# Retention attention ahead of two dense layers: quarter-array attention blocks and a finer share of dense work

## The chip, the cores and the metric

One Trainium2 chip, one core. The metric is device time in microseconds (us) for one execution of the whole program. TensorE (PE) multiplies, VectorE (DVE), ScalarE (ACT) and GpSimd (POOL) work on elements, SyncE (SP) issues most of the transfers.

## The reference

Three layers follow each other. The first is attention with a state that decays per head (batch 2, 8 heads, 768 tokens, 64 values per head); its output, 1536 tokens of 512 values, passes through two dense layers.

```python
state = gamma * state + k_t (outer) v_t          # per head, gamma = 1 - 2**(-5 - h)
y_t = (1 / sqrt(64)) * q_t @ state
...
h = x @ w_in;  x = (h * tanh(softplus(h))) @ w_out              # 512 -> 2048 -> 512
x = (sigmoid(x @ w_gate) * (x @ w_val)) @ w_out                 # 512 -> 1536 -> 512
```

All inputs and the output are float32.

## The kernel before

**Attention by blocks.** The 1536 tokens are 12 blocks of 128 (six for each batch). `load` brings `qk` and `nv` of a block (512 KB each), four blocks ahead. `at_prep` lets GpSimd scale the values (`vp`) and, except for the first block of a batch, the table of output scales (`og`). `at_scores` multiplies keys with queries, 64 rows of the array for each of the two heads of a pair and 128 outputs (`sc`), and VectorE masks the result (`a`). `at_state` adds keys times values into a state bank (`st`, K = 128 rows, 64 outputs), which ScalarE copies to `s` for the next block. `at_out` adds masked scores times values (`ao<-a,vp`, "inside") and queries times state (`ao<-qk_t,s`, "across", head 0 on rows and outputs 0 to 63, head 1 on 64 to 127) in one bank, and VectorE scales it into the layer's input `acc`. Each attention product is f32 and stands in the trace as two matmul instructions.

**Dense work.** A dense product of f32 accuracy is three matmuls with operands that are split in a rounded part and a remainder (`mm3`): ScalarE writes the rounded part, VectorE or GpSimd the remainder (`split`, `put`). Weights arrive packed (`raw`, 512 KB a piece) and are decoded by two ScalarE and two VectorE operations (`decode`). `plain1(i, c)` computes two tiles of the first layer for a chunk of 512 tokens; each tile is twelve matmuls of 512 columns. `mish` is ScalarE's activation, `put_g` splits its result.

**Order.** While `early` holds, every engine's queue follows the order of the Python calls. `blocks` goes through four attention blocks: scores of block j + 1, one step of weight preparation (`pump`), state and output of block j, the next loads, and then one dense tile. Chunk 0 is complete after block 3 (`put_plain` makes its split copies `xc`), chunk 1 after block 7 (`put_block`, `B11` and `B21`). So no dense work runs beside blocks 0 to 3, and one tile of twelve matmuls follows each of the eight later blocks. `flush` emits the rounded parts and remainders of weights that are due. After block 11 `early` is cleared: the rest of the program is recorded as a graph and `replay` issues it in an order found by list scheduling. Its first work is `out1(0, 0, G0)`, 48 matmuls with the weights `wo`; beside it GpSimd and ScalarE form the sums and differences of blocks (`T`, `B`, `YT`) which the later products need.

Of the kernel before, what the change touches and what calls it, by code (L numbers as in the profile page):

```python
# [23 lines left out]
def kernel(ctx, tc, qk, nv, w1i, w1o, w2g, w2v, w2o, ma_in, og_in, sg_in, ck_in, out):  # L24
# [26 lines left out]
    AHEAD = 4  # L51

# [213 lines left out]
    y_t = {n: big.tile([P, 2, 2, H], F32R, name="Y" + n) for n in ("T1", "T2", "T3")}  # L266
    y_t |= {"B11": xc_t[:, :2, :, :H], "B21": xc_t[:, 2:, :, :H], "T4": xc_t[:, :2, :, H:], "B22": xc_t[:, 2:, :, H:]}
# [47 lines left out]
    steps, late_hi, late_lo, sums_t, vs = [], [], [], {}, {}  # L315
# [51 lines left out]
    def put(key, v):  # L367
        t = slot(key)
        if home(key) == "q":
            v = v[:, H:]  # L370
        hi, lo = t[:, 0], t[:, 1]
        late_hi.append(lambda: act.activation(out=hi, in_=v, func=AF.Copy))
# [43 lines left out]
    def flush():  # L416
        flush_hi()
        while late_lo:
            late_lo.pop(0)()

    def pump(n=1):
        flush()
        for _ in range(n):
            if not steps and not plan():
                return
            ring = steps[0][0]
            if not room(ring) if ring else "dcs" not in lo_eng:
                return
            steps.pop(0)[1]()

    def weight(key):
        while key not in w_t:
            if not steps:
                assert plan(), key
            steps.pop(0)[1]()
        flush()
        return w_t[key]
# [45 lines left out]
    g_t = {}  # L483
# [94 lines left out]
    def plain_steps(key, done, halves=None, own=False):  # L578

        def one(i):  # L580
            o = hx["pool"].tile([P, N], F32, tag=f"x{i}", name="hx") if own and i in hx["own"] else hbank()
            w = weight(("a", *key, i))
            for kk in range(KK):
                xs, k = (xc_t, kk) if not halves else (b_t[halves[kk // 2]], kk % 2)
                mm3(o, lambda a: w[:, a, kk * P:kk * P + P], lambda b: xs[:, k, b, :], kk == 0, kk == KK - 1)
            spend(("a", *key, i))
            r[i] = o
            done(i, r)

        r = {}  # L590
        return [lambda: one(0), lambda: one(1)]

    def put_g(e, key):
        g = gp.tile([P, 2, N], F32R, tag="g", name="g")
        split(e, g[:, 0], g[:, 1], lo_eng["g"])
        g_t[key] = g

# [14 lines left out]
    def o1(i, c, d, k=2):  # L612
        o = hbank() if i == c == 0 else ps_o.tile([P, N], F32, tag="o", name="o")
# [63 lines left out]

    def out2(j, c):
        return seq([lambda s=s: o2(j, c, s) for s in range(SPC)])
# [27 lines left out]
    with ExitStack() as actx:  # L707
        ac = actx.enter_context(tc.tile_pool(name="ac", bufs=1))
        ld = actx.enter_context(tc.tile_pool(name="ld", bufs=AHEAD))
        at = actx.enter_context(tc.tile_pool(name="at", bufs=2))  # L710
        ps_s = actx.enter_context(tc.tile_pool(name="ps_s", bufs=1, space=PSUM))
        hx["pool"], hx["own"] = actx.enter_context(tc.tile_pool(name="ps_e", bufs=1, space=PSUM)), (0,)
        ma = ac.tile([P, 1, P], F32, name="ma")
        ck = ac.tile([P, SPB, 2 * NP, 1], F32, name="ck")
        sg = ac.tile([P, SPB, NP, 1], F32, name="sg")
        og0 = ac.tile([P, NP, P], F32, name="og0")
        qk_t, nv_t, a_t, vp_t, og_t, st_t, s_t = {}, {}, {}, {}, {}, {}, {}
# [8 lines left out]
        def at_prep(j):  # L726
            if j >= NSUB:
                return
            vp_t[j] = at.tile([P, 2 * NP, D], F32, tag="vp", name="vp")
# [3 lines left out]
            og_t[j] = og0  # L733
            if j % SPB:
                og_t[j] = at.tile([P, NP, P], F32, tag="og", name="og")
                pool.tensor_tensor(out=og_t[j], in0=og0, in1=sg[:, j % SPB].to_broadcast([P, NP, P]), op=ALU.mult)

        def at_scores(j):
            t = qk_t[j]
            sc = [ps_h.tile([P, NP, P], F32, tag="h", name="sc") for _ in range(2)]  # L740
            for p in range(NP):
                for e in range(2):
                    r = slice(D * e, D * e + D)
                    pe.matmul(out=sc[e][:, p, :], lhsT=t[r, 1, p, :], rhs=t[r, 0, p, :])
            a = at.tile([P, 2, NP, P], F32, tag="a", name="a")
            for e in range(2):
                dve.tensor_tensor(out=a[:, e], in0=sc[e], in1=ma.to_broadcast([P, NP, P]), op=ALU.mult)
            a_t[j] = a

        def at_out(j):  # L750
            a, v, t, s = a_t.pop(j), vp_t[j], qk_t[j], s_t.get(j)
            o = ps_o.tile([P, NP, P], F32, tag="o", name="ao")
            inter = j % SPB > 0

            for p in range(NP):
                for e in range(2):
                    pe.matmul(
                        out=o[D * e:D * e + D, p, :], lhsT=v[:, 2 * p + e, :], rhs=a[:, e, p, :],
                        start=p == 0, stop=p == NP - 1 and not inter, skip_group_check=True,
                    )  # L760
            if inter:
                for p in range(NP):
                    for e in range(2):
                        r = slice(D * e, D * e + D)
                        pe.matmul(
                            out=o[r, p, :], lhsT=s[r, p, :], rhs=t[r, 0, p, :], start=False, stop=p == NP - 1,
                            skip_group_check=True,
                        )
            dve.tensor_tensor(
                out=acc_t[j // SPC][:, :, j % SPC * P:j % SPC * P + P], in0=o, in1=og_t[j], op=ALU.mult  # L770
            )

        def at_state(j):
            if j % SPB == SPB - 1:
                return
            v, k = vp_t[j], nv_t[j]
            if j % SPB == 0:
                st_t[0] = ps_s.tile([P, NP, D], F32, tag="s", name="st")
            st = st_t[0]
            for p in range(NP):  # L780
                for e in range(2):
                    pe.matmul(
                        out=st[D * e:D * e + D, p, :], lhsT=k[:, 0, 2 * p + e, :], rhs=v[:, 2 * p + e, :],
                        start=j % SPB == 0 and p == 0, stop=p == NP - 1, skip_group_check=True,
                    )
            s_t[j + 1] = at.tile([P, NP, D], F32, tag="s", name="s")
            act.activation(out=s_t[j + 1], in_=st, func=AF.Copy)

        def fin(j):
            at_state(j)  # L790
            at_out(j)

        def blocks(j0, dense, made):

            for j in range(j0, j0 + SPC):
                if j + 1 < NSUB:
                    at_scores(j + 1)
                if j >= SPC - 1:
                    pump()
                fin(j)  # L800
                flush_hi()
                at_prep(j + 2)
                load(j + AHEAD)
                load_piece()
                if j == j0 + SPC - 1:
                    flush()
                    made()
                if dense:
                    dense.pop(0)()
            run(dense)  # L810

        for t, table in ((ck, ck_in), (ma, ma_in), (og0, og_in), (sg, sg_in)):
# [3 lines left out]
        z = at.tile([P, NP * D], F32, tag="s", name="z")  # L816
        dve.memset(ap=z, constant=0.0)
        for n in range(WARM):
            o = ps_o.tile([P, NP * D], F32, tag="o", name="warm")
            pe.matmul(out=o, lhsT=z[:, 0:P], rhs=z)  # L820
        for j in range(AHEAD):
# [4 lines left out]
        blocks(0, [], put_plain)  # L826
        blocks(SPC, plain1(0) + plain1(1), lambda: (put_block("B11", 1, 0), put_block("B21", 1, 2)))
        blocks(2 * SPC, plain1(0, 1) + plain1(1, 1), lambda: None)
# [8 lines left out]
    for n in ("T4", "B22", "T1", "T2", "T3"):  # L837
        b_t[n] = big2.tile([P, 2, 2, N], F32R, tag=n, name=n)

    put_block("T4", 2, 0)  # L840
    put_block("B22", 2, 2)
    run(side_sums(), out1(0, 0, G0))
# [38 lines left out]
def _tables(H, D, S, C):  # L881
# [3 lines left out]
    ma = np.arange(C)[None, None, :] >= np.arange(C)[:, None, None]  # L885
    pos = np.arange(S).reshape(S // C, C) - S // 2
# [4 lines left out]
    tables = (("ma", ma), ("og", og), ("sg", sg), ("ck", ck[..., None]))  # L891
# [42 lines left out]
```

## Time and profile before

| | |
|---|---|
| median of 3 timed runs | 591.86 us (591.84 to 592.0) |
| the profiled execution | 592.67 us, span 590.5 us |
| PE busy | 578.4 us (98%), 3342 matmul instructions |
| PE weight loads | 483.4 us (82%), beside the matmuls |
| DVE, ACT, POOL busy | 387.0 (66%), 294.9 (50%), 401.2 us (68%) |
| moved by DMA | 52.30 MB |
| granted TensorE clock, mean | 0.999 |

The page's first part gives the busy time of each engine; a busy PE is one with a matmul in flight, which does not mean that the array is full. The page cuts the span into 40 slices of 14.76 us: DMA is at 9, 9 and 7 tenths in the first three and at 4 tenths or less afterwards. Views used below: tables of busy time by stretch (with the count of instructions in brackets), instructions in order of time (runs of equal ones merged, with the idle time before them and what ended it), and groups of instructions with their mean duration.

### The profile page before, as it was taken

The numbers are of one execution on the slowest core, as the hardware profiler recorded it, in microseconds if no ns is written. First come the engines' busy times: TensorE is split into PE (matmuls) and PEld (weight loads), VectorE is DVE, ScalarE is ACT, GpSimd is POOL, SyncE is SP. The second block draws the span as 40 slices with busy tenths as digits, with TensorE's granted clock in tenths as the row PEclk, the third lists the DMA queues.
The fourth block names the chain that finished last, engine by engine and source line by source line (L and its number), as shares of the span: only waits on it lengthen the run. The fifth ranks groups of instructions, "written<-read, shape, count | busy, mean of one in ns | idle before, by whom it ended". The sixth has DMA issues, their size and how long they took to land.

```text
span 590.5 us, 8781 instructions
## 1 busy us (share of the span) xinstructions
PE 578.4 (98%) x3342; PEld 483.4 (82%) x3342; DVE 387.0 (66%) x540; ACT 294.9 (50%) x533; POOL 401.2 (68%) x344
## 2 busy tenths in 40 slices
PE   8999999999999999999999999999999999999997
PEld 6788878778888888888778778788888888888885
DVE  3899730167878775748883657887677677654564
ACT  1455556466666655346655556575254354340220
POOL 3566299999995846258999998997484484560120
PEclk9999999999999999999999999999999999999999
DMA  9974320023323231203220022333222222000004
GB/s 344 404 273 147 108 73 0 1 71 103 108 94 127 71 108 40 68 2 117 91 78 1 0 72 72 108 108 107 72 72 72 72 71 72 0 2 1 0 37 178
DMA packets 15593, 52.30 MB, mean 89 GB/s; under 512 B 1984, under 2 KB 2112, under 8 KB 15552
## 3 DMA queue, kind: packets, MB, share of 16 engines
q1 hardware_dynamic: 14976, 51.39, 25.2%
q8 instruction: 26, 0.43, 0.3%
q10 hardware_dynamic: 576, 0.36, 0.2%
q14 instruction: 15, 0.12, 0.1%
HBM read 48.60 MB, written 3.15 MB: 88 GB/s over the span
## 4 chain that ended last, share of the span: by engine, by line
PE 79%; POOL 10%; DMA 3%; DVE 3%; issue 2%; ACT 1%; SPq 0%; DVEq 0%; POOLq 0%; ACTq 0%
PE o L143 33%; PE h L143 27%; PE hx L143 16%; POOL t L143 3%; PE ao L143 2%; POOL g L143 2%; DMA raw<-w1i 2%; POOL T L143 2%; PE sc L143 1%; DMA qk_t<-qk 1%; POOL s L143 1%; POOL YT L143 1%; POOL B L143 1%; POOL ww L143 1%; PE st L143 1%
## 5 line engine op out<-in xcount | busy, mean ns | idle before, releaser
L143 POOL TENSOR_TENSOR g<-e,g 128x512 fp32r<-128x512 f32 x81 | 112.5, 1400 | 79.2 <-ACT g L143 74.6
L143 DVE TENSOR_TENSOR acc<-o,acc 128x512 f32<-128x512 f32 x132 | 90.8, 688 | 65.5 <-PE o L143 64.6
L143 PE MATMUL o<-g,wo 128*128 128x512 f32 x528 | 129.0, 393 | 0.2
L143 PEld LDWEIGHTS o<-g,wo 128*128 128x128 f32 x528 | 96.4, 188 | 21.8 <-DVE acc L143 2.6
L143 PE MATMUL o<-wo,g 128*128 128x512 f32 x432 | 108.8, 392 | 0.5 <-ACT acc L143 0.5
L143 PE MATMUL h<-B,ww 128*128 128x512 f32 x372 | 94.7, 391 | 0.1
L143 PE MATMUL h<-T,ww 128*128 128x512 f32 x360 | 91.9, 391 | 1.2 <-ACT acc L143 1.0
L143 PEld LDWEIGHTS o<-wo,g 128*128 128x128 f32 x432 | 78.1, 189 | 15.2 <-ACT acc L143 1.1
L143 POOL TENSOR_TENSOR ww<-s,ww 128x512 fp32r<-128x512 f32 x35 | 51.3, 1468 | 53.2 <-ACT ww L143 53.2
L143 DVE SCALAR_TENSOR_TENSOR raw<-raw 128x512 int32<-128x512 int32 x68 | 70.5, 1037 | 22.7 <-ACT raw L143 22.3
L143 PEld LDWEIGHTS h<-B,ww 128*128 128x128 f32 x372 | 68.7, 188 | 14.6 <-POOL B L143 0.5
L143 PEld LDWEIGHTS h<-T,ww 128*128 128x128 f32 x360 | 66.9, 188 | 16.6 <-ACT acc L143 1.5
L143 DVE SCALAR_TENSOR_TENSOR v<-v,raw 128x512 int32<-128x512 int32 x68 | 70.5, 1038 | 6.4 <-ACT v L143 3.9
L143 ACT ACTIVATE raw<-raw 128x512 int32<-128x512 uint8 x68 | 45.6, 673 | 42.8 <-DMA raw<-w2g 10.0
L143 ACT ACTIVATE e<-h 128x512 f32<-128x512 f32 x57 | 33.8, 593 | 58.0 <-PE h L143 35.7
L143 ACT ACTIVATE g<-e 128x512 fp32r<-128x512 f32 x84 | 51.7, 630 | 16.0 <-DVE e L143 14.8
L143 PE MATMUL hx<-xc,ww 128*128 128x256 f32 (+1 forms) x336 | 54.4, 299 | 1.1 <-DVE hx L143 0.8
L143 PEld LDWEIGHTS hx<-xc,ww 128*128 128x128 f32 x336 | 48.6, 190 | 6.7 <-DVE hx L143 1.2
L143 DVE TENSOR_TENSOR h<-h,u 128x512 f32<-128x512 f32 x54 | 37.6, 696 | 24.5 <-PE h L143 24.2
L143 ACT ACTIVATE v<-raw 128x512 f32<-128x512 f32 x68 | 44.9, 665 | 15.5 <-POOL s L143 11.3
L143 PEld LDWEIGHTS hx<-YT,ww 128*128 128x128 f32 x288 | 40.6, 190 | 7.5 <-DVE u L143 2.6
L143 PE MATMUL hx<-YT,ww 128*128 128x256 f32 x288 | 42.3, 283 | 2.7 <-DVE u L143 1.8
(80 smaller groups left out, 735.6 us busy)
## 6 DMA issues: line engine op xcount, KB each, us to landing
raw<-w1i SPq DMA_DIRECT2D x16, 512.0 KB, 3.3
raw<-w1o SPq DMA_DIRECT2D x16, 512.0 KB, 3.4
qk_t<-qk SPq DMA_DIRECT2D x12, 512.0 KB, 6.2
nv_t<-nv SPq DMA_DIRECT2D x12, 512.0 KB, 7.1
raw<-w2g SPq DMA_DIRECT2D x12, 512.0 KB, 3.3
raw<-w2v SPq DMA_DIRECT2D x12, 512.0 KB, 3.4
raw<-w2o SPq DMA_DIRECT2D x12, 512.0 KB, 3.4
out<-acc SPq DMA_DIRECT2D x12, 256.0 KB, 2.0
```

The costliest lines, as they stand in the source:

```text
L143: i = call(**kw)
```

## The change

A block from the fifth on is treated as two halves of 64 tokens: scores only inside a half, the state copied after every half, and "across" products with the state of the start of the batch to the half. Every product is then 64 rows, 64 outputs and 64 columns, a quarter of the array; the state and the scores of one half use the rows of that half, and the two heads of a pair the two halves of the outputs. In the host's layout and in the state the two heads of pairs 1 and 3 change places. `lanes` alternates products of two lists that lie on different row halves. The first four blocks keep whole blocks, but their "across" products use all four quarters in turn, on two banks.

The 32 quarter-tiles of dense work (three matmuls each) are shared out over nine rounds by `SHARE`. `load_piece` comes before the load of block 4, weight remainders go to GpSimd after block 4, the split of `g` is put off to the next round, the scale tables are made once for both batches, the split of chunk 0 is shared between VectorE and GpSimd, and the first 48 output products fill four banks in another order (`first1`).

```diff
+    SHARE = (4, 4, 3, 3, 2, 2, 4, 5, 5)
+    T = 4
...
-    y_t = {n: big.tile([P, 2, 2, H], F32R, name="Y" + n) for n in ("T1", "T2", "T3")}
...
-            split(acc_t[c][:, k0 + k], b_t[n][:, k, 0], b_t[n][:, k, 1], lo_eng["x"])
+            split(acc_t[c][:, k0 + k], b_t[n][:, k, 0], b_t[n][:, k, 1], pool if early and k0 else lo_eng["x"])
...
+        parts = [[lambda i=i, kk=kk: part(i, kk) for kk in range(KK)] for i in range(2)]
+        return parts[0] + parts[1] if early else [lambda s=s: run(s) for s in parts]
...
+        late_g.append(lambda: split(e, g[:, 0], g[:, 1], lo_eng["g"]))
+        if not early:
+            late_g.pop(0)()
...
+    def first1(c):
+        o = [hbank() for _ in range(KK)]
+        def part(m, d):
+            w, g = weight(("o", 1, m)), g_t[1, m, c]
+            mm3(o[d], lambda a: w[:, a, d * P:d * P + P], lambda b: g[:, b, :], m == 0, m == G0 - 1)
...
+        return seq([lambda m=m, d=d: part(m, d) for n in (0, 2) for d in range(KK) for m in (n, n + 1)])
...
+        def quarter(o, w, x, start=True, stop=True):
+            pe.matmul(out=o, lhsT=w, rhs=x, start=start, stop=stop, skip_group_check=True)
+        def scores(j, r):
...
+            def pair(p):
+                for s in range(2):
+                    quarter(sc[rows(s), p // 2, 2 * (p % 2) + (r + p) % 2, :], t[rows(r), 1, p, rows(s)],
+                            t[rows(r), 0, p, rows(s)])
+        def mask(j):
...
+            for r in range(2):
+                h = slice(r, NP - r, 3 - 2 * r)
+                dve.tensor_tensor(out=a[:, :, h], in0=sc_t.pop((j, r))[:, :, h, :],
+                                  in1=mh.to_broadcast([P, 2, NP // 2, Q]), op=ALU.mult)
+        def state(j, s):
...
+                for e in range(2):
+                    quarter(st[rows((e + p) % 2), p, :], k[rows(s), 0, 2 * p + e, :], v[rows(s), 2 * p + e, :],
+                            new and p == 0, p == NP - 1)
+        def keep(j, s):
+            s_t[2 * j + s + 1] = at6.tile([P, NP, D], F32, tag="s", name="s")
+            act.activation(out=s_t[2 * j + s + 1], in_=st_t[0], func=AF.Copy)
+        def outs(j, row):
...
+            def inside(p):
+                for e in range(2):
+                    quarter(o[rows(e), p, rows(row)], v[rows(row), 2 * p + e, :], a[rows(row), p // 2, 2 * (p % 2) + e, :],
+                            row == 0 and p == 0, False)
+            def across(p, s):
+                for m in range(2):
+                    quarter(o[rows((row + m) % 2), p + m, rows(s)], s_t[2 * j + s][rows(row), p + m, :],
+                            t[rows(row), 0, p + m, rows(s)], False, True)
...
+        def block(j, middle=lambda: None):
+            lanes(state(j + 1, 0) + scores(j + 1, 0), outs(j - 1, 1))
...
+            keep(j + 1, 0)
+            at_prep(j + 2)
+            middle()
+            while late_g:
+                late_g.pop(0)()
+            if j < NSUB - 1:
+                lanes(outs(j, 0), scores(j + 1, 1) + state(j + 1, 1))
+                mask(j + 1)
...
+            keep(j + 1, 1)
...
+        run(state(T, 0))
+        keep(T, 0)
+        lanes(scores(T + 1, 0), scores(T + 1, 1))
+        mask(T + 1)
+        run(state(T, 1))
+        keep(T, 1)
+        flush()
+        for k in range(KK):
+            split(acc_t[0][:, k], xc_t[:, k, 0], xc_t[:, k, 1], (dve, pool)[k % 2])
+        run(outs(T, 0), state(T + 1, 0))
+        keep(T + 1, 0)
+        at_prep(T + 2)
+        pump()
+        work(SHARE[0])
+        run(state(T + 1, 1))
+        keep(T + 1, 1)
+        load_piece()
+        lo_eng["w"] = pool
...
+        for j in range(T + 1, NSUB + 1):
+            block(j, lambda: (flush(), middles.get(j, lambda: None)()))
+            load(j + AHEAD - 1)
+            if j < NSUB and j != 2 * SPC:
+                feed()
+            work(SHARE[j - T])
...
-    run(side_sums(), out1(0, 0, G0))
+    run(side_sums(), first1(0))
```

## Rows read from the trace of the kernel before

**Rows 1.** The page's first part: engine, busy us, share of the span, instructions

```profile
PE 578.4 (98%) x3342; PEld 483.4 (82%) x3342; DVE 387.0 (66%) x540; ACT 294.9 (50%) x533; POOL 401.2 (68%) x344
```

**Rows 2.** Busy time by stretch: stretch, length, engines (count), clock, DMA share, GB/s

```profile
25.33:72.00 46.67, 46.35 (x483) 36.88 (x482) 42.61 (x54) 25.65 (x48) 24.19 (x18) 1.00 0.53 192
72.00:131.00 59.00, 56.51 (x257) 45.41 (x256) 17.43 (x19) 34.83 (x67) 56.85 (x53) 1.00 0.14 45
```

**Rows 3.** PE in order of time, one round: start us, us, operation, out<-in, shapes, count

```profile
47.31 1.16 PE L143 MATMUL sc<-qk_t 64*128 64x128 f32 x16
48.40 0.69 PE L143 MATMUL st<-vp,nv_t 128*64 128x64 f32 x16
48.91 1.05 PE L143 MATMUL ao<-a,vp 128*64 128x128 f32 x16
49.89 1.09 PE L143 MATMUL ao<-qk_t,s 64*64 64x128 f32 x16
50.91 3.01 PE L143 MATMUL hx<-B,ww 128*128 128x512 f32 x12
53.85 0.38 PE L143 MATMUL sc<-qk_t 64*128 64x128 f32 x2
```

**Rows 4.** Busy time by stretch, state group alone: first bracket counts matmuls in flight

```profile
41.94:41.95 0.01, 0.01 (x2) 0.01 (x4) 0.00 (x0) 1.00 1.99 819
41.96:41.96 0.00, 0.00 (x3) 0.00 (x5) 0.00 (x0) 1.00 0.00 0
41.97:41.98 0.01, 0.01 (x4) 0.01 (x6) 0.00 (x0) 1.00 0.00 0
42.02:42.03 0.01, 0.01 (x6) 0.01 (x6) 0.00 (x0) 1.00 0.00 0
```

**Rows 5.** The same for a scores group, with 128 columns

```profile
47.53:47.62 0.09, 0.09 (x4) 0.09 (x4) 0.00 (x0) 1.00 1.32 546
47.64:47.67 0.03, 0.03 (x6) 0.03 (x4) 0.00 (x0) 1.00 0.33 137
```

**Rows 6.** POOL in order of time, values of blocks 4 and 5 [idle before <-releaser]

```profile
18.89 1.04 POOL L143 TENSOR_TENSOR vp<-nv_t,ck 128x512 f32<-128x512 f32 x1 [2.07 <-DMA nv_t<-nv]
...
22.72 1.04 POOL L143 TENSOR_TENSOR vp<-nv_t,ck 128x512 f32<-128x512 f32 x1 [1.78 <-DMA nv_t<-nv]
```

**Rows 7.** PE in order of time, first dense product and the scores behind it

```profile
25.33 2.81 PE L143 MATMUL hx<-xc,ww 128*128 128x512 f32 x10
...
29.12 1.16 PE L143 MATMUL sc<-qk_t 64*128 64x128 f32 x16
```

**Rows 8.** PE in order of time, output products and the wait behind them

```profile
71.85 11.04 PE L143 MATMUL h<-g,wo 128*128 128x512 f32 x48
...
86.98 1.65 PE L143 MATMUL h<-T,ww 128*128 128x512 f32 x6 [1.03 <-ACT acc L143]
```

**Rows 9.** Groups of instructions, 25.3 to 72 us: busy us, mean ns | idle, releaser

```profile
L143 POOL TENSOR_TENSOR g<-e,g 128x512 fp32r<-128x512 f32 x7 | 10.0, 1424 | 14.5 <-ACT g L143 14.5
L143 DVE TENSOR_TENSOR a<-sc,ma 128x512 f32<-128x512 f32 x14 | 8.9, 677 | 0.0
...
L143 POOL TENSOR_TENSOR vp<-nv_t,ck 128x512 f32<-128x512 f32 x6 | 8.4, 1403 | 1.3 <-DMA nv_t<-nv 1.3
...
L143 ACT ACTIVATE g<-e 128x512 fp32r<-128x512 f32 x7 | 4.4, 631 | 0.2
...
L143 ACT ACTIVATE s<-st 128x256 f32<-128x256 f32 x6 | 2.2, 365 | 0.0
```

**Rows 10.** The tile nv_t from 30 us on: time from issue to landing

```profile
DMA to landing us min/median/max: 4.4/5.0/5.6
```

**Rows 11.** DVE and POOL in order of time, around the last block's end

```profile
71.00 0.68 DVE L143 TENSOR_TENSOR acc<-ao,og 128x512 f32<-128x512 f32 x1
...
73.45 1.29 POOL L143 TENSOR_TENSOR g<-e,g 128x512 fp32r<-128x512 f32 x1 [3.71 <-ACT g L143]
```

More of the change, by code (lines that the diff above doesn't have):

```diff
@@ new lines, in state, with pair @@
+        def state(j, s):
+            if j >= NSUB:
+                return [lambda: [quarter(st_t[0][rows(c), 0, :], z[rows(0), rows(0)], z[rows(0), rows(0)]) for c in range(2)]]
+            v, k = vp_t[j], nv_t[j]
+            new = j % SPB == 0 and s == 0
+            if new:
+                st_t[0] = ps_s.tile([P, NP, D], F32, tag="s", name="st")
+            st = st_t[0]
+            def pair(p):
+                for e in range(2):
+                    quarter(st[rows((e + p) % 2), p, :], k[rows(s), 0, 2 * p + e, :], v[rows(s), 2 * p + e, :],
+                            new and p == 0, p == NP - 1)
+            return [lambda p=p: pair(p) for p in range(NP)]
@@ new lines, in keep @@
+        def keep(j, s):
+            s_t[2 * j + s + 1] = at6.tile([P, NP, D], F32, tag="s", name="s")
+            act.activation(out=s_t[2 * j + s + 1], in_=st_t[0], func=AF.Copy)
+        def outs(j, row):
+            if not T <= j < NSUB:
+                return []
+            if row == 0:
+                o_t[j] = ps_o.tile([P, NP, P], F32, tag="o", name="ao")
+            a, v, t, o = a_t[j], vp_t[j], qk_t[j], o_t[j]
+            def inside(p):
[6 more added lines that the diff above has]
+                            t[rows(row), 0, p + m, rows(s)], False, True)
+            return [lambda p=p: inside(p) for p in range(NP)] + [
+                lambda p=p, s=s: across(p, s) for s in range(2) if (2 * j + s) % (2 * SPB) for p in (0, 2)]
@@ L750, in at_out @@
         def at_out(j):
-            a, v, t, s = a_t.pop(j), vp_t[j], qk_t[j], s_t.get(j)
-            o = ps_o.tile([P, NP, P], F32, tag="o", name="ao")
-            inter = j % SPB > 0
+            a, v, t, s = a_t.pop(j), vp_t[j], qk_t[j], s_t.get(2 * j)
+            o = [ps_o.tile([P, NP // 2, P], F32, tag="o", name="ao") for _ in range(2)]
             for p in range(NP):
@@ L782, in at_state @@
                     pe.matmul(
-                        out=st[D * e:D * e + D, p, :], lhsT=k[:, 0, 2 * p + e, :], rhs=v[:, 2 * p + e, :],
-                        start=j % SPB == 0 and p == 0, stop=p == NP - 1, skip_group_check=True,
-                    )
[L786 to L810, printed above, removed]
@@ L812, with lanes @@
-        for t, table in ((ck, ck_in), (ma, ma_in), (og0, og_in), (sg, sg_in)):
+                        out=st[rows((e + p) % 2), p, :], lhsT=k[:, 0, 2 * p + e, :], rhs=v[:, 2 * p + e, :],
+                        start=j == 0 and p == 0, stop=p == NP - 1, skip_group_check=True,
+                    )
+            s_t[2 * j + 2] = at6.tile([P, NP, D], F32, tag="s", name="s")
+            act.activation(out=s_t[2 * j + 2], in_=st, func=AF.Copy)
+        def lanes(*sides):
+            for n in range(max(map(len, sides))):
+                for side in sides:
+                    if n < len(side):
+                        side[n]()
@@ L813 @@
+        for t, table in ((ck, ck_in), (ma, ma_in), (og_t[0], og_in), (sg, sg_in), (mh, mh_in)):
             act.dma_start(out=t, in_=table)
@@ L820, with work, feed @@
             pe.matmul(out=o, lhsT=z[:, 0:P], rhs=z)
+        def work(n):
+            for _ in range(n):
+                dense.pop(0)()
+        def feed():
+            pump()
+            load_piece()
         for j in range(AHEAD):
@@ L825 @@
         at_scores(0)
-        blocks(0, [], put_plain)
-        blocks(SPC, plain1(0) + plain1(1), lambda: (put_block("B11", 1, 0), put_block("B21", 1, 2)))
-        blocks(2 * SPC, plain1(0, 1) + plain1(1, 1), lambda: None)
+        dense = plain1(0) + plain1(1) + plain1(0, 1) + plain1(1, 1)
+        for j in range(T):
+            at_state(j)
+            if j < T - 1:
+                at_scores(j + 1)
+            else:
+                lanes(scores(T, 0), scores(T, 1))
+                mask(T)
+            at_out(j)
+            if j == 0:
+                load_piece()
+            load(j + AHEAD)
+            if j:
+                load_piece()
+            at_prep(j + 2)
+            if j == T - 2:
+                pump()
+        flush_hi()
+        run(state(T, 0))
[4 more added lines that the diff above has]
+        keep(T, 1)
+        flush()
+        for k in range(KK):
[3 more added lines that the diff above has]
+        at_prep(T + 2)
+        pump()
+        work(SHARE[0])
+        run(state(T + 1, 1))
+        keep(T + 1, 1)
+        load_piece()
+        lo_eng["w"] = pool
+        middles = {2 * SPC: lambda: put_block("B11", 1, 0), 2 * SPC + 1: lambda: put_block("B21", 1, 2)}
+        for j in range(T + 1, NSUB + 1):
[4 more added lines that the diff above has]
+            work(SHARE[j - T])
+        flush()
+        lo_eng["g"] = dve
+        while late_g:
+            late_g.pop(0)()
+        assert not dense
         flush()
```

109 lines of the change are left out of this document (66 added, 43 removed).

## The prediction

> **What bounds the kernel now.** I read the engine table of the page first, then a table of engine time by stretch, then TensorE's instructions in order of time, then what VectorE, ScalarE and GpSimd wait for. The table says PE (TensorE) is busy 98% of the span [rows 1], and by stretch it is busy 46.35 of the 46.67 us from the first dense product to 72 us; in the next 59 us it lacks only 2.5 us [rows 2]. So the end is set by how much PE work there is; the other engines matter where they are made to be late. VectorE is busy 42.6 of the same 46.67 us, ScalarE 25.7, GpSimd 24.2 [rows 2]: they have little to give.
>
> One round of the attention part is plain to see [rows 3]: scores, state, inside, across and then twelve dense products, each starting where the last one lets go: 1.09, 0.51, 0.98 and 1.02 us, together 3.60 us of attention, and 2.94 us of dense work up to the next scores. The dense part is not touched in amount; the 3.60 us are what the change rewrites, for blocks 4 to 11.
>
> How fast a small matmul runs is read from counts of instructions in flight. In a state group (64 columns, two column halves of the array) the count stands at two, is three at 41.96 and four at 41.97, and six at 42.02 [rows 4]: two instructions start together, on two parts of the array, and the next two 0.058 us later (16 instructions, so 8 such steps, make up 0.47 of the group's 0.51 us). Scores, on two row halves, show the same with 128 columns: steps of 0.11 us, from four in flight to six [rows 5]. So column halves run beside each other and row halves run beside each other. Each f32 product is two such instructions (16 for the 8 products of a group).
>
> **The change part by part, against the profiled run** (592.67 us, span 590.5; the median of the timed runs is 591.86, so I take the difference from the median).
>
> *Quarters.* A 128-token block becomes two 64-token halves: 16 score, 16 state, 16 inside and 16 across products of 64 columns, 64 rows and 64 outputs, 128 instructions in place of 64. Emission alternates two lanes, one on each row half, and each step of a lane uses both column halves. If all four quarters run at once, a phase of 32 products (64 instructions) is 16 steps of 0.058 us, 0.93 us, and a block has two phases: 1.87 us instead of 3.60. The trace has no instruction that runs beside three others. The bounds are 0.93 us a phase (four at once) and 1.87 us (two at once, the state rate of rows 4). I take 0.93, because rows and columns each overlap without slowing the other and the steps stay at the streaming time; both ends are kept.
>
> *Form changes.* Groups of one form take 0.88 us for eight steps of 0.11, yet 0.98 to 1.09 us to the next group [rows 3, 5]: about 0.1 us for each change between tile forms. Before there are four a block; after it two (dense to quarters and back).
>
> *The start.* SP now sends a weight piece ahead of block 4. The loads are one line: GpSimd's scaled values of blocks 4 and 5 each wait for their nv load, 3.83 us apart [rows 6], which is three pieces of 512 KB (one weight, qk, nv) at 1.28 us. Block 4's values move from 18.89 to about 20.2, so its first state product cannot start before 21.2. Then state, scores 5, state and outputs follow (0.47 + 0.47 + 0.47 + 0.93 us and 0.2 us for the copy of the state), to 23.8. Block 5's nv lands at 22.7 as before (the same bytes stand ahead of it); its values are ready at 23.8, its state (0.47) ends near 24.4, and the first dense product comes at about 24.5 against 25.33 [rows 7]. The shorter across groups of blocks 1 to 3 (four at once, 0.44 for 0.88 us) save 1.3 us that this line of loads takes back: worth nothing.
>
> *From there to the output products*, PE alone: 32 parts of three products at 0.71 us (2.94 less one form change, a quarter of it), 22.7 us; one state half 0.47, fourteen phases 13.0, one single-lane phase 0.93, together 14.4; nineteen form changes 1.9. Sum 39.0 us: 24.5 + 39.0 = 63.5, where the kernel before starts them at 71.85 [rows 8].
>
> *Stalls*, which I expect to eat over half of that, because a round shrinks from 6.54 us to between 3.5 and 4.9 while the chains around it don't shrink:
> – Input split for the first dense product: the before kernel lost 0.85 us here (25.33 to 29.12 is 3.79, not 2.94) [rows 7]; the four copies now stand behind a state copy in ScalarE's queue, and half the remainders go to GpSimd. 0.9 us.
> – The state copy after the second half of block 5 has no cover: PE's next product writes the same bank. Result latency 0.2, copy 0.37 [rows 9], semaphores: 0.65 us.
> – Weights 1, 2 and 3 are each used in the round that finishes them. From the start of a phase: state half and latency 0.65, copy 0.37, rounding copy 0.63, and a remainder of about 1.42 on GpSimd, queued behind the 1.40 us scaling of a later block [rows 9]: 3.1 us. PE needs the remainder at the third product, 1.87 + 0.1 + 0.48 = 2.45. About 0.7 us, three times, and 0.2 more where that scaling itself waits for a load that takes 4.4 to 5.6 us [rows 10]: 2.3 us.
> – Rounds 8 to 10: ScalarE has mish, the rounding of g and two block copies (about 0.6 us each) ahead of the state copy PE waits for: 0.6 us twice, 1.2.
> Sum 5.05 us. The output products start at 63.5 + 5.05 = 68.6, which is 3.2 us earlier.
>
> *VectorE and GpSimd.* Masks (fourteen of 0.68 us in that stretch [rows 9]) halve; the seven later weight remainders leave VectorE for GpSimd; five late scale products leave GpSimd. So VectorE sheds about 10 us and GpSimd gains some 4: both fit in 44 us, and cost only through the queues above.
>
> *Handover.* What comes next waits for the last block and for GpSimd: the before kernel has the last block's values 0.2 us before the output products, the new one some 2 us before, behind five parts of dense work; GpSimd is free about 3 us into them in both [rows 11]; and PE lost only 1.03 us afterwards, on ScalarE [rows 8]. The four-bank order of the first output products has the same 48 matmuls. I give it zero, at most 1 us either way.
>
> **Forecast: 591.86 − 3.2 = 588.6 us.** By the stalls (half or one and a half times 5.05, and 0.5 for the handover) it lies between 586 and 591.
>
> **Rivals.**
> *Two at a time.* The queue feeds no more than the rows show, two instructions per 0.058 us. Every two-lane phase is 1.87, fourteen of them add 13.1 us; the longer rounds cover the weights and copies, leaving 1.6 us of stalls: 24.5 + 39.0 + 13.1 + 1.6 = 78.2, which is 6.3 us later: 598.2, slower. The sign turns at a mean of about 0.022 us an instruction (71.85 − 65.1 = 6.75 us over 896 instructions, on top of 0.0145). For it: no row has four. Against it: neither half slowed the other, and the second start of a pair follows within 0.02 us.
> *Between two and four.* A limit on the queue's starts that lies between: half way, 6.5 us more instead of 13.1, gives 71.6, no change.
> The Trainium skill, page "TensorE: Matmul & The Clock Gate", section "Wait — 56ns, not 53.3ns?", says that start-to-start never drops below about 25 ns however small the product. Taken over the whole engine, an estimate by that page is 14 × 64 × (0.025 − 0.0145) = 9.4 us more: 24.5 + 39.0 + 9.4 + 1.6 = 74.5, a result of 594.5. Rows 4 show one start between two counts 0.01 us apart, so here it could hold only as a floor for one part of the array.
> *The engines keep up.* Stalls three and four vanish, since VectorE is lighter and GpSimd's times are those under contention: 63.5 + 1.6 = 65.1, 585.1 us. For it: the before kernel's rounds show no PE wait. Against: its rounds are two thirds longer.
> *The short rounds choke.* Rounds 7 to 9 have two or three parts; loads are issued when the block four earlier is done, and landing (5.0) plus scaling (1.4) is 6.4 us, against two rounds of 3.5 and a phase. If these waits double all stalls, the output products start at 73.6: 593.6, slower.
>
> **Chances.** Forecast 0.52 (0.03 of it within 0.2% of before), engines keep up 0.17, choke 0.11 (0.04 within 0.2%), between two and four 0.07 (half within 0.2%), two at a time 0.13. Faster by over 0.2% (1.2 us, about what a measurement can tell from no change): 0.66; within 0.2%: 0.11; slower: 0.23. The range from 584.5 to 596 takes in all but the last case.
>
> **What would show it.** Right: in the new trace a two-lane phase of 64 instructions takes 0.93 to 1.0 us to the next group, four instructions start per 0.06 us, the first dense product comes near 24.5, PE idles before parts that use weights 1 to 3, and the 48 output products start near 68.6. Wrong: phases of 1.6 to 1.9 us; or phases of 0.95 with no idle time after 30 us (then the stalls were mine); or an earlier start of the output products that PE gives back before 130 us, waiting for GpSimd.

## The result and the profile after

The changed kernel takes 597.82 us (median of 6 runs, 596.2 to 598.46) against 591.93 us of the kernel before in the same comparison: a ratio of 1.0095, 95% interval 1.008 to 1.011. It is slower by 5.9 us; the forecast was 588.6, and the range ended at 596. The profiled execution took 598.42 us, its span is 596.6.

The page's engine table and the row of the granted clock, to be held against [rows 1]:

```profile
PE 576.1 (97%) x3898; PEld 481.2 (81%) x3898; DVE 380.2 (64%) x536; ACT 298.7 (50%) x545; POOL 408.5 (68%) x347
...
PEclk9989998999999999999999999999999999999999
```

The clock row of the kernel before:

```profile
PEclk9999999999999999999999999999999999999999
```

PE is busy 2.3 us less and the span is 6.1 us longer: the loss is mostly idle time. The clock row, at 9 tenths or more in every slice before, has dips in the third and in the seventh slice. TensorE of the kernel after in order of time (start us, us, operation, out<-in, shapes, count, in brackets idle time and what ended it; some runs of equal rows left out):

```profile
24.39 0.50 PE L146 MATMUL hx<-xc,ww 128*128 128x512 f32 x1
25.19 0.97 PE L146 MATMUL hx<-xc,ww 128*128 128x512 f32 x3 [0.30 <-DVE xc L146]
26.33 2.43 PE L146 MATMUL hx<-xc,ww 128*128 128x512 f32 x8 [0.18 <-POOL xc L146]
...
33.21 2.58 PE L146 MATMUL h<-xc,ww 128*128 128x512 f32 x10 [0.48 <-POOL ww L146]
...
35.73 0.27 PE L146 MATMUL st<-vp,nv_t 64*64 64x64 f32 x2
...
36.24 0.22 PE L146 MATMUL sc<-qk_t 64*64 64x64 f32 x2
36.25 0.23 PE L146 MATMUL ao<-qk_t,s 64*64 64x64 f32 x2
36.30 0.23 PE L146 MATMUL sc<-qk_t 64*64 64x64 f32 x2
36.31 0.23 PE L146 MATMUL ao<-qk_t,s 64*64 64x64 f32 x2
...
37.17 0.23 PE L146 MATMUL ao<-qk_t,s 64*64 64x64 f32 x2
...
37.75 0.73 PE L146 MATMUL hx<-xc,ww 128*128 128x512 f32 x2
41.27 3.35 PE L146 MATMUL hx<-xc,ww 128*128 128x512 f32 x7 [2.79 <-POOL ww L146]
...
54.27 0.27 PE L146 MATMUL st<-vp,nv_t 64*64 64x64 f32 x2 [0.59 <-POOL vp L146]
...
60.92 0.27 PE L146 MATMUL st<-vp,nv_t 64*64 64x64 f32 x2 [1.89 <-POOL vp L146]
...
76.13 11.04 PE L146 MATMUL h<-g,wo 128*128 128x512 f32 x48
88.09 1.66 PE L146 MATMUL h<-T,ww 128*128 128x512 f32 x6 [0.92 <-ACT acc L146]
...
93.52 0.73 PE L146 MATMUL h<-B,ww 128*128 128x512 f32 x2 [2.56 <-POOL B L146]
...
94.84 2.88 PE L146 MATMUL h<-T,ww 128*128 128x512 f32 x6 [0.58 <-ACT acc L146]
97.52 1.92 PE L146 MATMUL h<-B,ww 128*128 128x512 f32 x6
99.28 1.07 PE L146 MATMUL h<-T,ww 128*128 128x512 f32 x4
```

Three things stand here. The quarters run four at once: two instructions of one lane, two of the other 0.01 us later, the next four 0.058 us later; from 36.24 to 37.17 are 64 instructions in 0.93 us. A block takes 2.02 us (35.73 to 37.75) instead of 3.60. The dense part begins at 24.39, 0.94 us earlier than before [rows 7]. And then TensorE waits: at 41.27 for a weight remainder of GpSimd, at 54.27 and 60.92 for GpSimd's scaled values. The 48 output products start at 76.13, 4.28 us later than before [rows 8]. From there to the end are 520.5 us against 518.65 before, another 1.8 us.

GpSimd in order of time tells who is waited for:

```profile
38.51 1.04 POOL L146 TENSOR_TENSOR vp<-nv_t,ck 128x512 f32<-128x512 f32 x1 [4.10 <-DMA nv_t<-nv]
39.51 1.71 POOL L146 TENSOR_TENSOR ww<-v,ww 128x512 fp32r<-128x512 f32 x1
...
52.83 1.39 POOL L146 TENSOR_TENSOR vp<-nv_t,ck 128x512 f32<-128x512 f32 x1 [4.67 <-DMA nv_t<-nv]
...
59.31 1.56 POOL L146 TENSOR_TENSOR vp<-nv_t,ck 128x512 f32<-128x512 f32 x1 [2.17 <-DVE raw L146]
...
77.58 1.30 POOL L146 TENSOR_TENSOR wo<-v,wo 128x512 fp32r<-128x512 f32 x1 [7.45 <-ACT wo L146]
78.83 1.18 POOL L146 TENSOR_TENSOR t<-acc 128x256 f32<-128x256 f32 x1
```

GpSimd sits idle for 4.10 us ahead of the scaling of block 8 until its `nv` lands, and the weight remainder that TensorE wants is queued behind it: 39.51 + 1.71 = 41.22, and TensorE goes on at 41.27. The values of blocks 10 and 11 end at 54.22 and 60.87, and the state products start 0.05 us later each. (The row at 59.31 names VectorE; the load of block 11 lands at 59.15, so it was the load here too.) The tile `nv_t` from 30 to 62 us, time from issue to landing, beside [rows 10]:

```profile
DMA to landing us min/median/max: 6.1/6.5/7.5
```

In the kernel before no scaling waited for these loads. Issue and scaling of its block 8:

```profile
25.86 0.38 SPq L143 DMA_DIRECT2D nv_t<-nv  x1
...
39.35 1.50 POOL L143 TENSOR_TENSOR vp<-nv_t,ck 128x512 f32<-128x512 f32 x1
```

The load lands 6.9 us after its issue, at 32.7, which is 6.6 us ahead of its scaling; for blocks 9 to 11 it is 7.6 to 9.6 us. In the kernel after it is 0.2 us for blocks 8, 10 and 11, and 2.4 us for block 9.

Busy time in the stretch from 40 us (length, then PE, PEld, DVE, ACT, POOL, then clock, DMA share, GB/s):

```profile
40.00:47.50 7.50, 6.23 (x121) 5.10 (x125) 2.78 (x5) 0.90 (x2) 4.52 (x4) 0.54 0.54 181
```

Ahead of 40 us the granted clock is 1.00; here it is 0.54, mostly the 1.2 GHz level. It falls at about 40.3, while TensorE stands still (38.5 to 41.27), and is back at 47.2. The seven dense products at 41.27 take 3.35 us, from the second on 427 ns from start to start where 48 in 11.04 us [rows 8] are 230 ns each, and the next block 3.17 us (44.55 to 47.72) instead of 2.02.

### The profile page after: what moved, and what is told of

It reads as the page before. It is cut to its first block, busy times and chain, and to the rows that moved or that the text cites. A ratio compares the mean times of both kernels' runs of the same rounds, so it can differ in the third digit from the quotient of the medians.

```text
span 596.6 us, 9896 instructions
## 1 busy us (share of the span) xinstructions
PE 576.1 (97%) x3898; PEld 481.2 (81%) x3898; DVE 380.2 (64%) x536; ACT 298.7 (50%) x545; POOL 408.5 (68%) x347
## 4 chain that ended last, share of the span: by engine, by line
PE 79%; POOL 9%; DMA 5%; issue 2%; DVE 2%; ACT 1%; SPq 0%; POOLq 0%; DVEq 0%; ACTq 0%
PE o L146 35%; PE h L146 27%; PE hx L146 15%; DMA nv_t<-nv 5%; POOL t L146 1%; POOL vp L146 1%; POOL s L146 1%; POOL ww L146 1%; PE ao L146 1%; POOL B L146 1%; POOL YT L146 1%; POOL g L146 1%; POOL T L146 1%; PE st L146 1%; POOL xc L146 1%
## 5 line engine op out<-in xcount | busy, mean ns | idle before, releaser
L146 POOL TENSOR_TENSOR g<-e,g 128x512 fp32r<-128x512 f32 x78 | 108.4, 1400 | 60.5 <-ACT g L146 56.2
L146 DVE SCALAR_TENSOR_TENSOR raw<-raw 128x512 int32<-128x512 int32 x68 | 71.8, 1056 | 27.9 <-ACT raw L146 27.7
L146 DVE SCALAR_TENSOR_TENSOR v<-v,raw 128x512 int32<-128x512 int32 x68 | 69.0, 1016 | 5.4 <-ACT v L146 2.8
L146 PE MATMUL hx<-xc,ww 128*128 128x256 f32 (+1 forms) x336 | 56.8, 306 | 4.0 <-POOL ww L146 2.8
L146 POOL TENSOR_TENSOR wo<-v,wo 128x512 fp32r<-128x512 f32 x27 | 38.8, 1444 | 8.7 <-ACT wo L146 8.7
```

The lines of the kernel that those rows point to most:

```text
L146: i = call(**kw)
```

## Experiments

The theory after this trace: `nv` of a block is loaded too late for GpSimd's scaling, and GpSimd's queue, which works in order, passes the delay on to weight remainders and sums. The rivals: the order of GpSimd's queue alone; the quarters on TensorE; the new order of the output products. All runs of a group share their runs of the kernel before (591.93 us beside the kernel after, 592.0 for e1, e2, e4 and e6, 591.99 for the others). "Start" is that of the 48 output products, "rest" is from there to the end of the span, both of the one profiled run, which is the slowest of its kind for e1, e2, e4 and e5 and the fastest for e7 and c1_w_dve.

| run | us (median, range, runs) | ratio to before, 95% | start | rest |
|---|---|---|---|---|
| before | 591.93 to 592.0 | 1 | 71.85 | 518.65 |
| after | 597.82 (596.2–598.46, 6) | 1.0095 (1.008–1.011) | 76.13 | 520.5 |
| e1_nv_early | 592.07 (591.53–595.17, 10) | 1.0009 (0.9992–1.0026) | 71.18 | 521.9 |
| e2_weights_first | 598.99 (598.13–600.37, 4) | 1.0111 (1.0092–1.013) | 78.64 | 519.9 |
| e4_one_lane | 598.92 (597.2–600.45, 4) | 1.0114 (1.0088–1.014) | 76.09 | 522.5 |
| e6_flush_early | 593.34 (592.12–595.52, 10) | 1.0025 (1.001–1.0039) | 74.25 | 517.85 |
| e7_nv_first | 593.63 (591.39–596.31, 10) | 1.0032 (1.002–1.0045) | 69.30 | 520.3 |
| e3_w_dve | 591.63 (590.11–594.93, 10) | 0.9999 (0.9985–1.0012) | 71.92 | 518.5 |
| e5_out1 | 594.97 (593.9–595.6, 4) | 1.005 (1.0036–1.0064) | 72.45 | 521.35 |
| c1_both | 589.78 (589.12–590.67, 7) | 0.9967 (0.9955–0.9978) | 69.40 | 518.3 |
| c2_out1 | 588.92 (588.12–589.57, 5) | 0.9948 (0.9936–0.996) | 68.71 | 517.8 |
| c2_one_lane | 595.14 (595.07–595.16, 4) | 1.0052 (1.0039–1.0066) | 75.36 | 517.8 |
| c3_w_dve | 589.31 (588.86–590.55, 5) | 0.9957 (0.9944–0.9969) | 68.58 | 519.0 |
| c1_w_dve | 590.50 (589.48–591.54, 6) | 0.9973 (0.9962–0.9985) | 69.58 | 518.0 |

**The load earlier.** The changed kernel issues `nv` of block j + 3 in round j, behind `qk`, and scales it in round j + 1. Now `nv` of block j + 5 goes out at the end of round j, two rounds earlier; `nv` of blocks 8 and 9 goes out ahead of these rounds, and `qk` stays.

```diff
         keep(T, 1)
+        load_nv(T + AHEAD)
         flush()
...
             load(j + AHEAD - 1)
+            load_nv(j + 1 + AHEAD)
```

> The changed kernel with one thing moved: the nv load of a block is issued as soon as the second state half of the block four earlier has been multiplied, about one round sooner; qk stays where it is. Theory A (GpSimd's queue is held by a scaling that waits for a late nv, the weight remainder behind it comes late, TensorE idles and its clock drops): the 2.95 us idle at 41.3, the 0.75 and 2.05 us at 54.3 and 60.9 and the half clock after 41 us go, the output products start near 70 instead of 76.1, and the time is 591 (589.5 to 593). Theory B (GpSimd simply has too much work since it took over the weight remainders): the wait only changes its name, 596 to 598.

5.75 us less, and the start comes 4.95 us earlier, though the profiled run is the slowest of the ten (595.17 us) and its first dense products ran at the lower clock (about 25 to 29 us). The loads of blocks 8 to 11 go out 6.8 to 13.4 us earlier, which is more than the one round that the expectation gives it. GpSimd in order of time, for blocks 8 and 10:

```profile
37.56 1.04 POOL L146 TENSOR_TENSOR vp<-nv_t,ck 128x512 f32<-128x512 f32 x1 [2.20 <-issue]
38.56 1.29 POOL L146 TENSOR_TENSOR ww<-v,ww 128x512 fp32r<-128x512 f32 x1
...
46.98 1.04 POOL L146 TENSOR_TENSOR vp<-nv_t,ck 128x512 f32<-128x512 f32 x1 [2.06 <-issue]
```

No scaling in these rounds waits for a load any more (the loads land 6.5 to 8.5 us ahead of it, as in the kernel before), and TensorE's wait for the second weight is 0.48 us (at 39.90) instead of 2.79. The waits that the theory names go with the late load. On top of the edit of the handover (below) the same edit is worth 3.6 us, from 593.34 to 589.78. Whether one round earlier would do was not run.

**The load ahead of its neighbour.** `nv` of blocks 8 to 11 goes ahead of `qk`, nothing else.

```diff
-                sync.dma_start(out=qk_t[j], in_=qk[j])
-                sync.dma_start(out=nv_t[j], in_=nv[j])
+                for tile_, src_ in pair if j < 2 * AHEAD else pair[::-1]:
+                    sync.dma_start(out=tile_, in_=src_)
```

> The changed kernel with the two loads of each of blocks 8 to 11 exchanged: nv ahead of qk. nv should land 1.3 to 1.5 us sooner in four rounds, qk as much later, which has a round to spare. If the scaling that waits for nv, with the weight and the state products behind it, is what holds TensorE, 592.5 to 596. Rival: GpSimd has too much to do in a short round, and a load that is 1.4 us sooner only moves its wait: 597 to 598.5.

4.2 us less, within the expectation: the time goes with the landing of `nv`. The ten runs spread over 5 us; the profiled one is the fastest of them, with landings of 5.0 to 6.0 us. The load of block 8 also goes out 0.75 us earlier, no longer behind `qk`. The scalings of blocks 10 and 11 still wait for their load there (2.82 and 0.67 us).

**The order of GpSimd's queue alone.** The scaling is emitted behind the remainders of weights and of `g`.

```diff
-            at_prep(j + 2)
             middle()
             while late_g:
                 late_g.pop(0)()
+            at_prep(j + 2)
```

> The changed kernel with GpSimd's scaling of block j + 2 emitted behind the weight and g remainders of the round instead of ahead of them. Theory A: the idle of 2.95 us before the dense part at 41.3 and the half clock behind it go (4 to 5 us), but the state products of later blocks wait longer for their scaling (1 to 2 us more): 593.5 to 596. Theory B: the remainders are late in any order: 597 to 599.

No gain: the wait changes its place. TensorE of this run in order of time:

```profile
41.32 1.91 PE L146 MATMUL hx<-xc,ww 128*128 128x512 f32 x7 [0.30 <-POOL ww L146]
...
44.02 0.27 PE L146 MATMUL st<-vp,nv_t 64*64 64x64 f32 x2 [0.80 <-POOL vp L146]
```

The weights are almost in time (0.30 us instead of 2.79), and now the state products wait for scaled values, which GpSimd ends at 43.96:

```profile
41.21 1.31 POOL L146 TENSOR_TENSOR g<-e,g 128x512 fp32r<-128x512 f32 x1
42.46 1.50 POOL L146 TENSOR_TENSOR vp<-nv_t,ck 128x512 f32<-128x512 f32 x1
```

The load of this block was issued at 34.03 and landed 5.6 us later, at 39.62; the scaling starts 2.8 us after that, straight behind the remainder of `g`. Blocks 9 to 11 are scaled 1.4 to 2.2 us after their load has landed. So here the queue holds the scaling back and not the load: put in either order, something in this queue is late. The time lies where theory B had it (597 to 599).

**Weight remainders on VectorE.** One line of the change is undone.

```diff
-        lo_eng["w"] = pool
```

> The changed kernel with one part undone: the remainders of weights stay on VectorE after block 4. GpSimd's queue then holds no weight behind the scaling that waits for a load. Theory (TensorE waits for weight remainders that are queued behind a scaling that waits for its load): the waits for weights (about 0.7 and 3.0 us, and the 3.3 us that the half clock adds behind the long one) go, those of the state products for the scaling stay: 592.5 to 595. Rival (the late load alone sets the pace of a round, whoever makes the remainders): 596.5 to 598.5.

6.2 us less, more than expected. The waits for weights are gone; waits of the state products for scaled values stay (0.43 us at 45.55, 1.39 us at 51.85, 0.69 us at 56.24). So two parts of the change together make the loss, the late load and the weights behind it in one queue; either alone, taken back, is worth about 6 us. (The edit also takes work off GpSimd, which this run doesn't tell from the order in its queue. That GpSimd simply had too much work is answered by the last pair of runs: with the load early, the weights on GpSimd cost nothing that can be measured.)

GpSimd no longer waits for the last output weight at the handover, and its sums begin at 65.32, 6.6 us ahead of the output products. TensorE waits for `B` just as long as in the kernel after:

```profile
87.83 0.73 PE L146 MATMUL h<-B,ww 128*128 128x512 f32 x2 [2.58 <-POOL B L146]
89.15 1.66 PE L146 MATMUL h<-T,ww 128*128 128x512 f32 x6 [0.59 <-ACT acc L146]
90.64 1.54 PE L146 MATMUL h<-B,ww 128*128 128x512 f32 x6
92.02 1.52 PE L146 MATMUL h<-T,ww 128*128 128x512 f32 x6
```

But the granted clock stays at 1.00 here: the twelve products behind the wait take 2.87 us (89.15 to 92.02), where the kernel after, at the lower clock from 94.9 to 98.3, takes 4.44 us for them (94.84 to 99.28). That is 1.6 of the 2.0 us by which the rest is shorter (518.5 for 520.5).

**The quarters at half rate**, once in the changed kernel and once without the late load: the lists of a phase one behind the other instead of alternating.

```diff
-            for n in range(max(map(len, sides))):
-                for side in sides:
-                    if n < len(side):
-                        side[n]()
+            for side in sides:
+                for f in side:
+                    f()
```

> The changed kernel with the two lanes emitted one after the other, so that products on the two row halves no longer alternate and at most two quarters run at once. If the four-at-once rate is what carries the attention part: a phase goes from 0.94 to 1.87 us, fourteen phases add 13 us of TensorE work, of which longer rounds win back up to 9 us of waits: 601 to 606. If the waits set the pace whatever the products cost: 597 to 599.

> The version with the early nv load, the early last weight and the old order of output products, and now at most two quarters at once: the lists of products come one after the other instead of alternating (as one of the earlier runs did with the changed kernel, where it cost 1 us). If, once the late load is gone, TensorE's own work sets the length of a round, thirteen phases grow from 0.93 to about 1.87 us, 12 us, less some 2 us of waits that longer rounds cover: 597 to 601. Rival: chains through the other engines still set the length of a round, and the quarters' speed is hidden: 589 to 591.5.

In the changed kernel it costs 1.1 us, with intervals that overlap, and the start stays where it was (76.09, 76.13 in the kernel after): TensorE's speed in the quarters is hidden behind the chain. In the kernel without the late load it costs 6.2 us. That lies between the two ranges of the expectation, and is less than the 12 us I had put on a pure two-at-a-time order. TensorE of that run shows why:

```profile
37.71 0.68 PE L146 MATMUL st<-vp,nv_t 64*64 64x64 f32 x16
38.22 0.46 PE L146 MATMUL sc<-qk_t 64*64 64x64 f32 x10
38.47 0.27 PE L146 MATMUL ao<-a,vp 64*64 64x64 f32 x2
38.51 0.28 PE L146 MATMUL sc<-qk_t 64*64 64x64 f32 x3
...
40.84 1.52 PE L146 MATMUL hx<-xc,ww 128*128 128x512 f32 x4
```

The block takes 3.13 us (37.71 to 40.84), not 3.9: products of the second list, which stand behind all of the first in the queue, start beside its last ones (38.47). So the speed of the quarters shows in the time once the late load is gone, and hardly before.

**The handover.** The last weight's rounded part is emitted ahead of the last five parts of dense work:

```diff
+            if j == NSUB:
+                flush()
             work(SHARE[j - T])
```

> The changed kernel with the rounded part and remainder of the last output weight emitted ahead of the last five dense parts, not behind them. In the changed kernel GpSimd sat idle for 7.45 us until ScalarE, behind the last mish, had rounded that weight, and its sums for the later products began at 78.8. If this late start is what makes TensorE wait at 88 to 98 us (1.1, 2.7, 0.7 us and a half clock): 593 to 595. If the order that the list scheduling gave GpSimd's sums makes the waits: 597 to 598.

In the changed kernel ScalarE rounds that weight behind the last activation (76.39), GpSimd waits 7.45 us for it and begins its sums at 78.83, 2.7 us into the output products; in the kernel before it begins them 2.9 us into them, straight behind other work [rows 11]. Here the rest is 517.85 us, 2.6 less: the wait for `B` is 1.95 us instead of 2.56, and the clock stays up behind it. The start is also 1.9 us earlier, in rounds whose code is unchanged; the loads landed at other times. So not all of the 4.5 us by which the median falls can be put down to the edit. Both edits together:

> Both single edits together: the nv load of a block is issued one round earlier, and the last weight's rounded part and remainder are emitted ahead of the last five parts of dense work instead of behind them. If the late load (5.8 us alone) and the idle GpSimd at the handover (4.5 us alone) are separate losses, the gains add up to most of their sum: 587.5 to 590.5 us, faster than the kernel before. Rival: both runs removed the same delay (a GpSimd that falls behind in the rounds and is still behind at the handover), and then the two together give no more than the larger: 591 to 592.5.

589.78: the larger part of the sum, and faster than before.

**The order of the output products** goes back to that of the kernel before, first in the changed kernel, then on top of both edits.

```diff
-    run(side_sums(), first1(0))
+    run(side_sums(), out1(0, 0, G0))
```

> The changed kernel with one part undone: the 48 output products in the order and banks of the kernel before. If the order costs what the handover lost, 594 to 596. Rival: the handover is lost because GpSimd waits 7.5 us for ScalarE's rounding of the last output weight, whatever order the products have: 597 to 598.5.

> The same two edits, and the 48 output products go back to the order and the banks of the kernel before. If the new order of these products is what makes the sums late against TensorE (2.7 us of idle time before the first product that uses B in all runs so far, and half clock behind it), this gives 3 to 6 us more than the two edits alone: 583 to 587. Rival: the order is indifferent and the sums are late because GpSimd's share of them is unchanged; then it is within 1 us of the two edits alone.

On top of both edits the wait of 1.95 us for `B` goes (no wait ahead of 100 us is over 0.4 us), but waits of 0.71 and 1.30 us come up at 106.8 and 123.4, and the rest differs by 0.5 us (518.3 to 517.8), as the rival had it. In the changed kernel the time falls by 2.85 us, into the range for an order that costs, but the rest is 0.9 us longer: what was gained lies ahead of these products, in code that is the same in both, where the loads landed at other times. So the order is not shown to make the kernel slower, and a gain of 3 us can come without any edit to the rounds or the loads. It is not shown to be free either: the order of before is the faster one in all three pairs (by 2.85, 0.9 and, below, 1.2 us), and in the pairs with both edits its runs have a granted clock of 0.997 to 1.000 over the span, those with the new order 0.993 to 0.997. With the order of before, c2_out1 is the fastest. TensorE in it, in order of time:

```profile
39.23 1.88 PE L146 MATMUL hx<-xc,ww 128*128 128x512 f32 x7 [0.48 <-POOL ww L146]
...
68.71 11.04 PE L146 MATMUL h<-g,wo 128*128 128x512 f32 x48
```

and GpSimd ahead of the handover:

```profile
64.55 1.28 POOL L146 TENSOR_TENSOR wo<-v,wo 128x512 fp32r<-128x512 f32 x1 [2.09 <-ACT wo L146]
65.78 0.74 POOL L146 TENSOR_TENSOR t<-acc 128x256 f32<-128x256 f32 x1
```

The sums begin 2.9 us ahead of the output products, and the seven products that took 3.35 us take 1.88.

**Both, with the weights on VectorE too**, with either order:

> The version with the early nv load, the early last weight and the old order of output products (588.9), and the remainders of weights stay on VectorE. What is left of waits for GpSimd in the rounds is 0.64 us twice (weights) and 0.75 and 0.48 us (scaled values): with the weights off GpSimd's queue 587.0 to 588.5. Rival: VectorE, busy with decoding and masks, makes the remainders as late as GpSimd did, or is late with a mask: 588.9 to 591.

> The same with the new order of the output products. In the pair without and with the old order (589.8 and 588.9) the time from the start of these products to the end differed by 0.5 us only: what the new order waits for at B it gets back before 130 us. If that holds, this is within 1 us of the version with the old order, 587.0 to 589.5. Rival: the order matters by itself, and with the half clock behind the wait at B it costs 2 us or more: 589.5 to 591.5.

No further gain: 0.4 and 0.7 us more than with the weights on GpSimd, and the intervals overlap. Both times lie in the ranges of the rivals. Once the load is early, which of the two engines makes the remainders makes no difference clear of the noise.

## Why the prediction was wrong, by its steps

**Quarters: right.** 0.93 us a phase, 2.02 us a block (1.87, and 0.15 for two changes of form). The rival of two at a time is refuted, and the one between two and four with it. The Trainium skill, page "TensorE: Matmul & The Clock Gate", section "Wait — 56ns, not 53.3ns?", would have starts no closer than about 25 ns; over the whole array they are 14.6 ns apart on the mean here (64 in 0.93 us), and only within one quarter are they further apart than that (0.058 us).

**The start: right**, 24.39 for 24.5.

**Stalls: the step that failed.** For a scaling that waits for its load the sum had 0.2 us, inside the weights' term, and nothing for the state products behind such a scaling or for the clock. From 24.39 to 76.13 are 51.74 us; less the 39.0 us of TensorE alone that is 12.7, not 5.05. By terms of the profiled runs (a wait counts with 0.16 us more than the idle time in the rows, because a next product can start 0.23 us after one that is in flight for 0.39 us):

| term | forecast | after | c2_out1 |
|---|---|---|---|
| input split | 0.9 | 1.4 | 1.4 |
| state copy without cover | 0.65 | 0.75 | 0.75 |
| weights 1 to 3 | 2.3 | 0.65 + 2.95 | 0.64 + 0.64 |
| ScalarE, rounds 8 to 10 | 1.2 | none named | none named |
| state products behind late values | – | 0.75 + 2.05 | 0.48 |
| clock at the lower level | – | 2.6 | 0 |
| a wait inside a block, no engine named | – | 0.9 | – |
| what is left, not named | – | 0.7 | 1.2 |
| sum | 5.05 | 12.7 | 5.1 |

(The clock's 2.6 us: from the dense products at 41.27 up to the next block 3.28 us instead of 1.81 in c2_out1, and 3.17 instead of 2.02 us for that block.) The last column is a check: with `nv` earlier and the two edits at the handover, the stalls are 5.1 us and the start is 68.71, where the forecast had 5.05 and 68.6. The size of the sum was right for a kernel whose loads are in time, but its terms differ (0.9 for 1.4, 2.3 for 1.3, 1.2 for none), so part of that agreement is luck.

What I misread is one line of the rival of choking rounds: landing and scaling, 6.4 us, "against two rounds of 3.5 and a phase". The kernel before issues `load(j + 4)` in round j and scales that block in round j + 2: two rounds of 6.5. The changed one issues `load(j + 3)` in round j and scales block j + 3 in the first half of round j + 1: one round, and a shorter one. The rival had the right mechanism, with a chance of 0.11 and the price of doubled stalls (593.6). The price was too low three times over: landing was 6.1 to 7.5 us, not 5.0; the scaling that waits holds up the weights queued behind it, so waits add up along GpSimd's queue; and a wait of almost 3 us was followed by 3 to 7 us at half the clock, for which no term stood.

**VectorE and GpSimd "cost only through the queues": right in words, and not followed up.** The queue was the cost: with the weights left on VectorE the changed kernel takes 591.63.

**Handover: wrong.** I had zero, at most 1 us; it was 1.8, and 1.6 of that is the lower clock behind the wait for `B`, for which no term stood either. That "GpSimd is free about 3 us into them in both" was read rightly (2.7 and 2.9 us). But the second `B` is ready 17.3 us into the output products (92.21 + 1.26) instead of 13.3 (83.86 + 1.30), with the first sums at 1.18 instead of 0.73 us each and `B` behind more of them. With the sums begun earlier (e3_w_dve, e6_flush_early, c1_both, c2_out1) the loss is gone, but in e3_w_dve the wait for `B` is as long as ever and only the clock differs. How much of the wait is the order and how much the slower sums isn't settled.

## What to carry to other kernels

When a change shortens a round, count for each load how many rounds lie between its issue and its first reader, before and after, and on which in-order queue that reader stands: there the load's lateness is handed on to everything behind it. A faster TensorE stage is worth its gain only if its feeders are moved earlier by as much; here the kernel with the same quarters takes 1% more than before with the late load, as much as before with that load issued earlier, and 0.5% less with two more edits at the handover. A forecast that prices each wait alone is too low where one queue serves several of them.

## What the runs showed of the hardware that was not expected

- f32 products on four quarters of the array run at once without slowing each other, and a product waiting further back in the queue starts on a free quarter beside earlier ones (38.47 above, where six of the instructions ahead of it start from 38.51 to 38.64).
- The granted clock fell to the 1.2 GHz level for stretches of 3.4 to 6.8 us, in the kernel after behind waits of 2.8 and 2.6 us; 427 ns between dense products where 230 are usual. A wait of that length doesn't always bring it: behind 2.58 us in e3_w_dve the clock stayed at 1.00. It isn't tied to long waits alone either: in c1_both the dense products from 25.43 on ran so (to 28.8) behind the small products of the attention part and an idle time of 0.31 us, and in c2_out1, with the same code up to there, they didn't. What decides it stays open.
- The loads of `nv` of blocks 8 to 11, 512 KB each and issued right behind `qk`, landed 6.1 to 7.5 us after their issue, against 4.4 to 5.6 for blocks 9 to 11 before, and differently in kernels with the same code up to there (5.8 to 6.4 us in e5_out1, start 72.45 for 76.13). Why is not shown. The kernels with one part undone and ten runs spread over 3.4 to 4.9 us, those with both edits over 2.1 at most in their five to seven.
